# Prefix decays written to DRAM once per chunk, and a new order of the work, in an mLSTM layer with two MLPs

## The chip, the core and the metric

The kernel runs on one core of one Trainium2 chip. The metric is the device time of one execution in microseconds (us); three runs of the kernel before gave 461.3, 463.23 and 463.48 us, median 463.23.

## The reference

An mLSTM attention layer for 2 batches, 8 heads, 768 steps and head size 40 is followed by two MLPs (320 to 2048 to 320) over the 1536 tokens, the first with a hard-swish, the second with a mish.

```python
for t in range(S):
    m_new = np.maximum(f_gate[:, :, t] + m, i_gate[:, :, t])
    f_stab = np.exp(f_gate[:, :, t] + m - m_new)
    i_stab = np.exp(i_gate[:, :, t] - m_new)
    C = f_stab * C + i_stab * outer(vt, kt)
    n = f_stab * n + i_stab * kt
    y[:, :, t] = sigmoid(o_gate[:, :, t]) * (C @ qt) / np.maximum(np.abs(n . qt), 1.0)
x = y as (1536, 320)
h = x @ w1_in;  x = (h * clip(h + 3, 0, 6) / 6) @ w1_out
h = x @ w2_in;  out = (h * tanh(log1p(exp(h)))) @ w2_out
```

## The kernel before

The steps are cut into 6 chunks of 128 (`c` from 0 to 5); a chunk of one batch is a *unit* `(b, c)`. `gates(c)` (L665) transposes the gates of a chunk, forms the decay of each step, and with one scan along the chunk the product of the decays up to each step, the *prefix decays*: 16 rows (batch and head) of 128 values in `mt`. They go to a DRAM tile `pd` (L706 to 708), each row written 40 times, once for every element of a head, and come back per unit as `pb` (L773 to 777): 120 partitions (three heads of 40) in three groups, at rows 0, 120 and 200. `query` (L862) multiplies the transposed queries `q3` by `pb`, so that the product with the carried state `c` (L937, the tile `o`) has the decay since the chunk's start. The tiles `q3` and `pb` have one buffer each (`in_q3`), which L937 of the unit before sets free.

Of a unit, `scores` (L799) multiplies queries and keys (tile `s`), `decays` (L817) makes the 128 by 128 decay matrices of its 8 heads with a scan (tile `fb`; the row that it starts from is loaded from DRAM, `fz`, or for the first two chunks spread by TensorE at L831), `values` and `carry` (L844, L874) scale values and keys, form the state's new part (tile `st`, L888) and add it, and `unit` (L913) sums it all up in `o` (L937, L941), divides, gates, and transposes the result into the MLP's input `X` (tile `xp`).

The weights come as two pieces per slot of 256 features, `ri` (384 KiB each) and `ro` (320 KiB), into two raw buffers (`narrow`, L347, DMA at L357). Each piece is widened on ScalarE and VectorE (`top`, L365 and L367), rounded to the fast matmul's format on ScalarE (`wh`, `wd`) and has its remainder taken (`wl`, and the second half of `wd`) on VectorE, GpSimd or, where `pe_rest` says so, TensorE (`low_on_pe`, L384). The first MLP runs for chunks 0 and 1 in steps of 256 tokens (`ph` at L460, then `r`, `gh`, `gl`, then `acc` at L479), between the units of attention; for chunks 2 to 5 in steps of 512 tokens (`phw`, `accw`); then the second MLP (`qh`, `bcc`). Each of its steps is 8 matmuls up and 6 to 12 down.

All is recorded by a planner, `Flow` (L193): each task asks for an engine with an estimated duration, and the task with the lowest number in the table `P` goes first among those that are ready by the estimates. Every engine then runs its instructions in the order so recorded, and waits where the real durations differ. All DMAs are issued by SyncE (SP), in one row. Where TensorE has nothing to do by the estimates before the third unit's end, the planner puts products of zeros (`pz`, `fill` at L1122), which keep it busy.

Of the kernel before, what the change touches and what calls it, by code (L numbers as in the profile page):

```python
# [8 lines left out]
F32 = mybir.dt.float32  # L9
# [30 lines left out]


P = {
    "const": [140, 266, 278, 196, 64],
    "gates": [74, 143, 41, 167, 142, 225],
    "load": [233, 138, 177, 125, 222, 205, 154, 122, 158, 239, 102, 159],
    "score": [20, 32, 85, 37, 301, 314, 268, 110, 202, 161, 5, 223],
    "value": [72, 16, 305, 136, 251, 23, 197, 262, 248, 307, 117, 0],
    "carry": [105, 214, 215, 261, 67, 12, 260, 8, 137, 267, 9, 168],
    "unit": [96, 269, 232, 40, 124, 77, 257, 220, 38, 17, 242, 116],
# [8 lines left out]
    ],  # L58
    "down2": [
        203, 59, 171, 252, 4, 25, 156, 69, 6, 28, 147, 108, 180, 186, 34, 241, 35, 115, 80, 128, 55, 91,  # L60
        275, 19, 66, 18, 60, 224, 81, 86, 7, 151, 33, 118, 255, 250, 213, 30, 89, 73, 62, 53, 42, 56,
        134, 97, 319, 36,
    ],
    "half": [
        98, 13, 308, 263, 258, 221, 208, 279, 162, 39, 21, 298, 84, 240, 316, 112, 135, 90, 325, 54,
        119, 88, 201, 157,
    ],
    "wide1": [
        187, 150, 247, 297, 75, 99, 58, 153, 286, 169, 165, 245, 127, 193, 191, 277, 166, 270, 121, 284,
        139, 120, 311, 131, 285, 292, 68, 309, 306, 246, 276, 317,  # L70
    ],
    "down1w": [
        271, 289, 100, 148, 50, 101, 52, 65, 179, 234, 45, 173, 182, 175, 1, 238, 303, 94, 79, 57, 206,
        130, 43, 210, 61, 302, 172, 155, 93, 107, 82, 330,
    ],
    "drain": [322, 228, 326, 3, 27, 26, 2, 109, 76, 46],
    "now": [10, 14],
    "window": [0.01],


    "on_value": [1, 1, 1, 1, 0, 1, 0, 0, 0, 2, 0, 2],
    "on_key": [1, 2, 2, 1, 0, 1, 0, 1, 2, 1],
    "on_gate": [2, 1, 0, 1, 2, 0, 0, 0, 0, 0, 0, 0],
    "pool_query": [0, 0, 1, 0, 0, 0, 0, 0, 1, 0, 0, 1],
    "pool_state": [0, 0, 0, 1, 0, 0, 0, 0, 0, 0],
    "pool_rest": [
        1, 0, 1, 0, 0, 1, 0, 0, 1, 1, 0, 0, 0, 0, 1, 0, 0, 0, 0, 0, 0, 0, 0, 0, 0, 0, 0, 1, 1, 0, 0, 0,
    ],
    "pool_low": [
        0, 0, 0, 1, 0, 0, 1, 1, 0, 0, 0, 0, 0, 0, 0, 1, 1, 1, 0, 0, 0, 0, 0, 0, 0, 0, 1, 0, 1, 0, 0, 0,  # L90
        0, 0, 1, 0, 1, 1, 0, 1, 0, 0, 0, 0, 0, 0, 0, 0,
    ],

    "pe_rest": [0, 0, 0, 0, 0, 0, 0, 0, 0, 0, 0, 0, 0, 0, 0, 0],

    "pool_scan": [0, 0],

# [201 lines left out]
def mlstm_mlp_kernel(ctx, tc, qk, q3g, kvon, gates_io, w1i, w1o, w2i, w2o, eye, halves, consts, out):  # L299
# [368 lines left out]
    def gates(c):  # L668
        yield next(e for e, (_, z) in zip(scanned, SCANS) if c < z)
        yield have["ident"]  # L670
        q = slice(c * L, (c + 1) * L)
        yield in_a
        p = bank(f"pg{c}")
        yield PE, 0.21, 128
        T.transpose(p[:, 0:16], fgt[:, q], ident[:16, :16])
        T.transpose(p[:, 16:32], igt[:, q], ident[:16, :16])
        g = istab[c] = gpool.tile([128, 32], F32, tag=f"ist{c}", name=f"ist{c}")
        s = gpool.tile([128, 32], F32, tag=f"s{c}", name=f"s{c}")
        yield ACT, 0.16
        A.activation(s, p[:, 0:32], AF.Sigmoid, scale=-1.0)  # L680
        A.activation(g, p[:, 0:32], AF.Sigmoid)
        flow.put(in_a)
        yield DVE, 0.27
        V.reciprocal(out=s, in_=s)
        yield DVE, 0.1, True
        tt(V, g, g, s, ALU.mult)
        flow.set(gated[c])
        if c == 0:
            yield DVE, 0.03
            V.memset(g[0:1, 0:16], 0.0)  # L690
            flow.set(spreadable[c])
            return
        yield in_a
        pf = bank(f"pf{c}")
        yield PE, 0.11, 64
        T.transpose(pf[:16, 0:128], g[:, 0:16], ident)
        if P["spread"][c]:
            yield DVE, 0.03
            V.memset(g[0:1, 0:16], 0.0)
            flow.set(spreadable[c])  # L700
        yield ACT, 0.165
        A.copy(fgt[:, q], pf[:16, 0:128])
        yield DVE, 0.33, True
        V.tensor_tensor_scan(out=mt[:, q], data0=fgt[:, q], data1=fgt[:, q],
                             initial=1.0, op0=ALU.mult, op1=ALU.min)
        pd[c] = dpool.tile([16, D, L], F32, tag=f"pd{c}", name=f"pd{c}")  # L706
        yield SP, 330e3, rows_out[c][0]
        SY.dma_start(out=pd[c], in_=mt[:, q].unsqueeze(1).to_broadcast([16, D, L]))
        if not P["spread"][c]:
            yield DVE, 0.02  # L710
            V.memset(fgt[:, c * L : c * L + 1], 0.0)
            fzd[c] = dpool.tile([16, L], F32, tag=f"fz{c}", name=f"fz{c}")
            yield SP, 8e3, rows_out[c][1]
            SY.dma_start(out=fzd[c], in_=fgt[:, q])
        yield have["cst"]
# [13 lines left out]
    state = [gpool.tile([120, 3, 123], F32, tag=f"c{b}", name=f"c{b}") for b in range(B)]  # L729
    cnew = gpool.tile([120, 3, 123], F32, tag="cnew", name="cnew")  # L730
    units = [(b, c) for c in range(NC) for b in range(B)]
    got = {u: {k: Event() for k in ("qk", "kvo", "buf", "f", "q3", "p0", "p1")} for u in units}
    for u in units:
        got[u]["qk"] = Event(), Event()
    done = {u: {k: Event() for k in ("q3", "state", "o", "sig", "value")} for u in units}
# [4 lines left out]
    def loads(u, before):  # L740
# [29 lines left out]
        yield SP, 184e3, ev["q3"]  # L770
        SY.dma_start(out=t["q3"], in_=q3g[b, c])
        yield rows_out[c][0]
        rows = pd[c].rearrange("r e t -> (r e) t")[b * DM : (b + 1) * DM]  # L773
        yield SP, 123e3, ev["p0"]
        SY.dma_start(out=t["pb"][:, 0:2, :], in_=rows[0:240].rearrange("(g p) t -> p g t", g=2))
        yield SP, 61e3, ev["p1"]
        SY.dma_start(out=t["pb"][:, 2, :], in_=rows[200:320])

    def scaled(on, us, x, scale, n):

        if on == 2:
            yield ACT, H * (0.092 + 0.0007 * n)
            for h in range(H):
                A.mul(x[:, h, :], x[:, h, :], scale[:, h, :])
        else:
            yield flow.elementwise(on, us, H * n)
            tt(G if on else V, x, x, scale.to_broadcast([128, H, n]), ALU.mult)
# [9 lines left out]
    def scores(u):  # L797
        b, c = u
        t = tiles[u]  # L799
        for p in range(2):  # L800
            yield got[u]["qk"][p]
        yield got[u]["buf"]
        yield spreadable[c] if P["spread"][c] else got[u]["f"]
        yield in_pair
        yield in_a
        yield in_a
        flow.put(in_pair)
        sp = t["s"] = [bank(f"s{b}_{c}_{p}") for p in range(2)]
        yield PE, 1.06, 4096
        for h in range(4):  # L810
            for p in range(2):
                qke = t["qke"][64 * p : 64 * p + D]
                T.matmul(sp[p][:, h * L : (h + 1) * L], qke[:, 1, h, :], qke[:, 0, h, :], start=True, stop=True)  # L813
# [471 lines left out]
```

## Time and profile before

| | |
|---|---|
| median of three runs | 463.23 us |
| the profiled execution, its own time | 459.94 us |
| its span, first to last instruction | 458.2 us |
| TensorE busy (share of the span) | 441.1 us (96%) |
| VectorE, ScalarE, GpSimd busy | 317.7, 293.0, 54.1 us |
| DMA | 45.22 MB, of which 41.12 MB read from DRAM and 3.64 MB written |

The profile is of the one execution with its own time in the table; its span leaves out some 1.7 us around the instructions. A matmul's busy time is modelled and runs on into the next one's, so the distance between two starts tells what a matmul costs, and a busy TensorE may still run at half its clock: the granted clock is a row of its own. Single-precision matmuls appear as two records each, those in the fast format as one. SPq are the issue instructions of the DMA queue.

### The profile page before, as it was taken

To read this page: it belongs to the slowest core of one execution; us is meant where nothing else is said; L and a number is where in the kernel's file an instruction comes from. 1 tells how busy PE (TensorE), PEld (TensorE's weight loads), DVE (VectorE), ACT (ScalarE), POOL (GpSimd) and SP (SyncE) were. 2 spreads that over 40 slices of the span, in tenths; PEclk is the share of its full clock that TensorE was granted. 3 is DMA by queue.
4 is the path that set the end of the run, shared out by engine and by line. 5 is a ranking of instruction groups with operands and counts; after the bars stand their busy time and mean duration, and the time that the engine had idled before them with its cause. 6 is when DMAs were issued, how large, how long until landed. Compare 5 with 4: busy or idle time off the path is not lost.

```text
span 458.2 us, 7086 instructions
## 1 busy us (share of the span) xinstructions
PE 441.1 (96%) x2662; PEld 392.1 (86%) x2662; DVE 317.7 (69%) x552; ACT 293.0 (64%) x576; POOL 54.1 (12%) x53
## 2 busy tenths in 40 slices
PE   6987999699999999999999999999999999999996
PEld 5967999589999888888888888899989999889986
DVE  4796786669988777566555865766666666666665
ACT  4674683556747644766566666776777766767764
POOL 4323200132013301011024020000000000000000
PEclk9897899799999999999999999999999999999999
DMA  7768456895751652035203510000001000010001
GB/s 232 231 197 260 124 158 140 269 284 142 252 181 72 195 171 94 1 117 172 91 0 132 178 69 3 0 1 0 1 0 59 0 3 0 17 43 1 0 1 57
DMA packets 19636, 45.22 MB, mean 99 GB/s; under 512 B 1938, under 2 KB 11954, under 8 KB 19602
## 3 DMA queue, kind: packets, MB, share of 16 engines
q1 hardware_dynamic: 19602, 44.77, 31.1%
q8 instruction: 21, 0.34, 0.3%
q14 instruction: 13, 0.11, 0.1%
HBM read 41.12 MB, written 3.64 MB: 98 GB/s over the span
## 4 chain that ended last, share of the span: by engine, by line
PE 85%; DVE 5%; DMA 4%; ACT 2%; SPq 2%; issue 1%; POOL 0%; POOLq 0%; DVEq 0%; ACTq 0%
PE qh L460 19%; PE phw L460 13%; PE accw L479 13%; PE bcc L1091 6%; PE bcc L1090 6%; PE bcc L1089 6%; PE acc L479 5%; PE ph L460 5%; PE o L941 4%; PE s L813 2%; PE o L937 2%; DMA qke<-in_qk 1%; DMA pd<-mt 1%; PE st L888 1%; DMA ro<-in_w1o 1%; DMA pb<-pd 1%
## 5 line engine op out<-in xcount | busy, mean ns | idle before, releaser
L1091 PE MATMUL bcc<-wd,gl 128*128 128x320 f32 x192 | 59.3, 309 | 0.2 <-DVE gl L1046 0.2
L1089 PE MATMUL bcc<-wd,gh 128*128 128x320 f32 x192 | 59.3, 309 | 0.0
L1090 PE MATMUL bcc<-wd,gh 128*128 128x320 f32 x192 | 59.2, 309 | 0.0
L1040 DVE SCALAR_TENSOR_TENSOR u<-u,qh 128x512 f32<-128x512 f32 (+1 forms) x49 | 33.1, 676 | 36.8 <-ACT u L1038 36.8
L460 PE MATMUL qh<-xh,wh 128*128 128x512 f32 x144 | 56.8, 395 | 0.0
L460 PE MATMUL qh<-xl,wh 128*128 128x512 f32 x144 | 56.7, 393 | 0.0
L1036 ACT ACTIVATE u<-u,two 128x512 f32<-128x512 f32 (+1 forms) x49 | 35.1, 716 | 31.6 <-DVE u L1034 31.6
L479 PE MATMUL accw<-ghw,wd 128*128 128x512 f32 x160 | 52.2, 391 | 0.0
L1030 ACT ACTIVATE u<-qh 128x512 f32<-128x512 f32 (+1 forms) x49 | 28.7, 588 | 15.4 <-PE qh L460 15.4
L1089 PEld LDWEIGHTS bcc<-wd,gh 128*128 128x128 f32 x192 | 36.0, 188 | 2.1
L460 PE MATMUL qh<-xh,wl 128*128 128x512 f32 x96 | 37.7, 393 | 0.0
L460 PE MATMUL phw<-xh,wh 128*128 128x512 f32 x96 | 37.7, 393 | 0.0
L1090 PEld LDWEIGHTS bcc<-wd,gh 128*128 128x128 f32 x192 | 36.0, 188 | 1.9
L479 PE MATMUL accw<-glw,wd 128*128 128x512 f32 x96 | 37.5, 390 | 0.0
L479 PE MATMUL acc<-gh,wd 128*128 128x256 f32 x160 | 33.5, 295 | 4.1 <-ACT gh L549 4.1
L460 PE MATMUL phw<-xl,wh 128*128 128x512 f32 x96 | 37.4, 390 | 0.0
L1091 PEld LDWEIGHTS bcc<-wd,gl 128*128 128x128 f32 x192 | 36.0, 188 | 0.4 <-DVE gl L1046 0.4
L1046 DVE SCALAR_TENSOR_TENSOR gl<-u,gh 128x512 fp32r<-128x512 f32 (+1 forms) x49 | 33.1, 675 | 4.1 <-ACT gh L1044 4.0
L479 PEld LDWEIGHTS accw<-ghw,wd 128*128 128x128 f32 x160 | 29.8, 188 | 6.1
L1034 DVE SCALAR_TENSOR_TENSOR u<-u 128x512 f32<-128x512 f32 (+1 forms) x49 | 33.4, 682 | 1.6
L544 ACT ACTIVATE rw<-phw,half 128x512 f32<-128x512 f32 x32 | 22.0, 689 | 18.8 <-PE phw L460 15.1
L546 DVE SCALAR_TENSOR_TENSOR rw<-rw,phw 128x512 f32<-128x512 f32 x32 | 22.0, 686 | 16.3 <-ACT rw L544 16.2
(145 smaller groups left out, 1036.6 us busy)
## 6 DMA issues: line engine op xcount, KB each, us to landing
ri<-in_w1i SPq DMA_DIRECT2D x8, 768.0 KB
ri<-in_w2i SPq DMA_DIRECT2D x8, 768.0 KB
kvo<-in_kvon SPq DMA_DIRECT2D x12, 484.0 KB
ro<-in_w1o SPq DMA_DIRECT2D x8, 640.0 KB
ro<-in_w2o SPq DMA_DIRECT2D x8, 640.0 KB
fb<-fz SPq DMA_DIRECT2D x8, 512.0 KB
qke<-in_qk SPq DMA_DIRECT2D x24, 160.0 KB
out<-ot SPq DMA_DIRECT2D x12, 160.0 KB
```

The lines of the kernel that those rows point to most:

```text
L460: T.matmul(ph, a, b, start=(i == 0), stop=(i == len(seq) - 1))
L479: T.matmul(acc[k], a, b, start=start, stop=stop, skip_group_check=True)
L544: A.activation(r, ph, AF.Relu, bias=half, scale=1.0 / 6.0)
L546: V.scalar_tensor_tensor(out=r, in0=r, scalar=1.0, in1=ph, op0=ALU.min, op1=ALU.mult)
L1030: A.activation(u, ph, AF.Exp)
L1034: V.scalar_tensor_tensor(out=u, in0=u, scalar=2.0, in1=u, op0=ALU.add, op1=ALU.mult)
L1036: A.activation(u, u, AF.Ln, bias=two)
L1040: V.scalar_tensor_tensor(out=u, in0=u, scalar=0.5, in1=ph, op0=ALU.subtract, op1=ALU.mult)
L1046: V.scalar_tensor_tensor(out=gl, in0=u, scalar=-2.0, in1=gh.bitcast(F32), op0=ALU.mult, op1=ALU.subtract)
L1089: T.matmul(acc, a, hi, start=st, stop=False)
L1090: T.matmul(acc, a, lo, start=False, stop=False)
L1091: T.matmul(acc, b, hi, start=False, stop=sp)
```

## The change

It has three parts.

1. `pd` is now 16 rows of 128 values: one DMA of 8 KiB per chunk in place of one of 320 KiB. `pb` is loaded by three DMAs per unit (one per group) in place of two; each reads three rows of `pd`, every row 40 times by a step of zero, into 120 partitions. The bytes that arrive in `pb` are the same.
2. Two estimates of the planner: eight small ScalarE operations in `scaled` are now taken as 8 x (0.187 + 0.0007 n) us in place of 8 x (0.092 + 0.0007 n), and the scores count 2048 columns in place of 4096. The planner now also sees the three loads.
3. All numbers of the table `P` are new: the order, and where some operations run. `pe_rest` has two entries set (the first `ri` and the `ro` of slot 3 take their remainder on TensorE), `pe_low` one more, `pool_scan` one, and about as many operations as before are on GpSimd and on ScalarE's small scalings (7 each time).

```diff
-        pd[c] = dpool.tile([16, D, L], F32, tag=f"pd{c}", name=f"pd{c}")
-        yield SP, 330e3, rows_out[c][0]
-        SY.dma_start(out=pd[c], in_=mt[:, q].unsqueeze(1).to_broadcast([16, D, L]))
+        pd[c] = dpool.tile([16, L], F32, tag=f"pd{c}", name=f"pd{c}")
+        yield SP, 8e3, rows_out[c][0]
+        SY.dma_start(out=pd[c], in_=mt[:, q])
...
-        rows = pd[c].rearrange("r e t -> (r e) t")[b * DM : (b + 1) * DM]
-        yield SP, 123e3, ev["p0"]
-        SY.dma_start(out=t["pb"][:, 0:2, :], in_=rows[0:240].rearrange("(g p) t -> p g t", g=2))
-        yield SP, 61e3, ev["p1"]
-        SY.dma_start(out=t["pb"][:, 2, :], in_=rows[200:320])
+        rows = pd[c][b * H : (b + 1) * H]
+        for g in range(3):
+            yield SP, 61e3, ev[f"p{g}"]
+            src = rows[GBASE[g] : GBASE[g] + 3].unsqueeze(1).to_broadcast([3, D, L])
+            SY.dma_start(out=t["pb"][:, g, :], in_=src)
...
-            yield ACT, H * (0.092 + 0.0007 * n)
+            yield ACT, H * (0.187 + 0.0007 * n)
...
-        yield PE, 1.06, 4096
+        yield PE, 1.06, 2048
...
+        yield got[u]["p2"]
...
-    "pe_rest": [0, 0, 0, 0, 0, 0, 0, 0, 0, 0, 0, 0, 0, 0, 0, 0],
+    "pe_rest": [1, 0, 0, 0, 0, 0, 0, 1, 0, 0, 0, 0, 0, 0, 0, 0],
```

Two places of the order matter below. In the names, `s0_1` is unit (0, 1), `ph0_1` the first MLP's step for chunk 0 and slot 1; the number at a name's end is the program's count. A unit's eight matmuls of `s`, sixteen of a `ph` and of an `acc` are shown by their first or last row.

TensorE, from the scores of unit (0, 1) to its `o`, before (`o` is L937 and L941):

```order
L813 MATMUL s0_1_1_425<-qke0_1_293 128x128
L1122 MATMUL pz_151<-zeros_150 128x512 x12
L888 MATMUL st0_1_458<-kvo0_1_389 120x123 x3
L831 MATMUL fb1_1_0_479<-ident4_85,ist1_345 128x128 x4
L831 MATMUL fb1_1_1_480<-ident4_85,ist1_345 128x128 x4
L937 MATMUL o0_1_498<-c0_100,q30_1_398 128x123 x2
L941 MATMUL o0_1_498<-kvo0_1_389,fb0_1_395 128x41 x8
L813 MATMUL s1_1_0_510<-qke1_1_453 128x128
L460 MATMUL ph0_0_514<-xh0_92,wh0_0_123 128x256
L937 MATMUL o1_1_595<-c1_101,q31_1_531 128x123 x2
L941 MATMUL o1_1_595<-kvo1_1_476,fb1_1_478 128x41 x8
```

and now (the lines behind the change are one higher):

```order
L813 MATMUL s0_1_1_436<-qke0_1_312 128x128
L460 MATMUL ph0_0_453<-xh0_92,wh0_0_123 128x256
L1123 MATMUL pz_151<-zeros_150 128x512 x7
L831 MATMUL fb1_1_0_501<-ident4_85,ist1_358 128x128 x4
L460 MATMUL ph0_1_502<-xh0_92,wh0_1_129 128x256
L813 MATMUL s1_1_1_539<-qke1_1_483 128x128
L479 MATMUL acc0_541<-gh0_0_481,wd0_0_125 128x256 x2
L938 MATMUL o0_1_582<-c0_100,q30_1_415 128x123 x2
L942 MATMUL o0_1_582<-kvo0_1_401,fb0_1_412 128x41 x8
L831 MATMUL fb1_1_1_551<-ident4_85,ist1_358 128x128 x4
L889 MATMUL st0_1_526<-kvo0_1_401 120x123 x3
L938 MATMUL o1_1_677<-c1_101,q31_1_606 128x123 x2
```

Two steps up (`ph0_0`, `ph0_1`), the scores of unit (1, 1) and one step down (`acc`) now stand ahead of the first `o` that needs `pb`; before, filler, `st` and `fb` stood there, and the steps up came behind it. The next `o`, of unit (1, 1), is the last row shown: `fb`, `st` and two steps of 16 matmuls (`acc`, `ph0_2`) lie between.

SP, the loads around chunk 2's decays, before:

```order
L357 DMA ro1_0_751<-in_w2o 128x2560
L708 DMA pd2_749<-mt_99 640x1x128
L714 DMA fz2_770<-gio_98 16x128
L766 DMA fb0_2_675<-fz2_770 128x1024
L708 DMA pd4_834<-mt_99 640x1x128
L708 DMA pd3_838<-mt_99 640x1x128
L771 DMA q30_2_850<-in_q3g 120x384
L714 DMA fz4_860<-gio_98 16x128
L714 DMA fz3_872<-gio_98 16x128
L775 DMA pb0_2_851<-pd2_749 120x2x128
L777 DMA pb0_2_851<-pd2_749 120x128
L357 DMA ro0_5_904<-in_w1o 128x2560
```

and now:

```order
L357 DMA ro0_5_653<-in_w1o 128x2560
L357 DMA ri0_3_778<-in_w1i 128x3072
L357 DMA ro1_0_799<-in_w2o 128x2560
L708 DMA pd2_840<-mt_99 16x128
L708 DMA pd5_851<-mt_99 16x128
L714 DMA fz5_874<-gio_98 16x128
L708 DMA pd3_876<-mt_99 16x128
L766 DMA fb0_2_748<-fz2_858 128x1024
L714 DMA fz3_910<-gio_98 16x128
L771 DMA q30_2_930<-in_q3g 120x384
L777 DMA pb0_2_931<-pd2_840 120x1x128 x3
L357 DMA ri0_4_952<-in_w1i 128x3072
```

The weight piece `ro` of slot 5 stood behind three writes of `pd`, the writes of `fz` and the loads of `pb`; it now stands ahead of them all, and `ri` of slot 4 stands behind them. A `pd` has 16 rows instead of 640, a `pb` three loads.

## Rows read from the trace of the kernel before

**Rows 1.** The page: busy time by engine; granted TensorE clock in 40 slices, tenths.

```profile
PE 441.1 (96%) x2662; PEld 392.1 (86%) x2662; DVE 317.7 (69%) x552; ACT 293.0 (64%) x576; POOL 54.1 (12%) x53
...
PEclk9897899799999999999999999999999999999999
```

**Rows 2.** Busy time in a stretch (from:to, us, engines with instruction counts, granted clock, DMA share, GB/s).

```profile
40.00:50.00 10.00, 10.00 (x57) 9.70 (x57) 5.25 (x12) 2.96 (x7) 4.21 (x4) 0.53 0.50 169
```

**Rows 3.** Chain that ended last, 27 to 52 us: start, us, what.

```profile
27.07 5.86 DMA pd<-mt
...
33.36 3.92 DMA pb<-pd
...
37.44 1.53 POOL q L306
...
39.01 1.43 PE o L937 x6
40.45 3.34 PE o L941 x16
...
45.80 5.65 PE ph L460 x32
```

**Rows 4.** Timeline of TensorE in the same stretch: start, us, what, idle before it.

```profile
30.99 3.04 PE L1122 MATMUL pz<-zeros 128*128 128x512 f32 x12
...
34.50 1.95 PE L831 MATMUL fb<-ident,ist 128*128 128x128 f32 x16
39.01 1.43 PE L937 MATMUL o<-c,q 120*128 120x123 f32 x6 [2.56 <-POOL q L306]
```

**Rows 5.** Chain that ended last, 114 to 122 us, TensorE at full clock.

```profile
114.15 1.92 PE ph L460 x16
116.06 1.09 PE s L813 x16
...
119.26 0.63 PE st L888 x6
119.89 0.64 PE o L937 x6
120.53 1.75 PE o L941 x16
```

**Rows 6.** Timeline of SP, the DMA issues after writes of `pd`.

```profile
28.54 2.47 SPq L357 DMA_DIRECT2D ro<-in_w1o  x1
...
69.44 3.24 SPq L771 DMA_DIRECT2D q<-in_q3g  x1
72.78 4.01 SPq L714 DMA_DIRECT2D fz<-gio  x2
...
79.07 0.36 SPq L357 DMA_DIRECT2D ro<-in_w1o  x1
```

**Rows 7.** Timelines of ScalarE (first row) and TensorE, 83 to 92 us.

```profile
83.27 0.91 ACT L365 CAST top<-ro 128x640 f16<-128x640 bf16 x1 [5.67 <-DMA ro<-in_w1o]
...
84.70 0.80 PE L479 MATMUL acc<-gh,wd 128*128 128x256 f32 x2 [4.08 <-ACT gh L549]
...
89.57 2.31 PE L941 MATMUL o<-kvo,fb 128*128 128x41 f32 x16
```

**Rows 8.** The page: DMA packets of the whole run.

```profile
DMA packets 19636, 45.22 MB, mean 99 GB/s; under 512 B 1938, under 2 KB 11954, under 8 KB 19602
```

**Rows 9.** Two more stretches, columns as in rows 2.

```profile
72.00:74.00 2.00, 2.00 (x18) 1.98 (x18) 2.00 (x3) 0.20 (x1) 0.00 (x0) 1.00 0.70 89
...
172.00:173.00 1.00, 1.00 (x9) 0.77 (x6) 1.00 (x3) 0.00 (x0) 1.00 (x1) 1.00 1.06 428
```

**Rows 10.** Timelines of SP and VectorE: the first DMA's issue and its user.

```profile
0.73 0.73 SPq L1106 DMA_DIRECT2D gio<-in_gates_io  x1
...
2.93 0.47 DVE L658 TENSOR_TENSOR_SCAN mt<-gio,mt 16x128 f32<-16x128 f32 x1 [2.02 <-DMA gio<-in_gates_io]
```

**Rows 11.** Groups by line: the query product (busy us, mean ns, idle before).

```profile
L306 DVE TENSOR_TENSOR q<-q,pb 120x384 f32<-120x384 f32 x7 | 3.8, 546 | 6.0 <-DMA pb<-pd 6.0
```

More of the change, by code (lines that the diff above doesn't have):

```diff
@@ L42 @@
 P = {
[L43 to L49, printed above, removed]
[4 rows of a table removed]
+    "const": [265, 317, 315, 178, 133],
+    "gates": [21, 23, 84, 212, 267, 172],
@@ L54 @@
+    "load": [203, 239, 304, 202, 135, 258, 66, 54, 87, 19, 260, 63],
+    "score": [229, 183, 217, 134, 113, 75, 311, 121, 147, 112, 266, 218],
+    "value": [128, 41, 247, 153, 318, 242, 106, 167, 302, 28, 92, 287],
+    "carry": [206, 104, 288, 291, 86, 208, 143, 148, 8, 137, 149, 52],
+    "unit": [211, 82, 176, 10, 39, 150, 55, 295, 117, 200, 131, 96],
[4 rows of a table added]
     "up2": [
[3 rows of a table removed]
[3 rows of a table added]
     ],
     "down2": [
-        203, 59, 171, 252, 4, 25, 156, 69, 6, 28, 147, 108, 180, 186, 34, 241, 35, 115, 80, 128, 55, 91,
@@ L61 @@
-        275, 19, 66, 18, 60, 224, 81, 86, 7, 151, 33, 118, 255, 250, 213, 30, 89, 73, 62, 53, 42, 56,
-        134, 97, 319, 36,
+        226, 94, 42, 5, 49, 132, 190, 164, 111, 81, 74, 145, 26, 227, 38, 61, 234, 76, 37, 51, 45, 22,
+        3, 244, 27, 58, 72, 68, 184, 25, 162, 158, 278, 71, 136, 36, 241, 182, 233, 139, 163, 171, 69,
+        130, 213, 220, 102, 165,
     ],
     "half": [
-        98, 13, 308, 263, 258, 221, 208, 279, 162, 39, 21, 298, 84, 240, 316, 112, 135, 90, 325, 54,
-        119, 88, 201, 157,
+        48, 12, 186, 316, 289, 57, 210, 245, 98, 232, 204, 271, 31, 142, 105, 314, 16, 181, 215, 294,
@@ L67 @@
+        299, 324, 256, 127,
     ],
     "wide1": [
-        187, 150, 247, 297, 75, 99, 58, 153, 286, 169, 165, 245, 127, 193, 191, 277, 166, 270, 121, 284,
-        139, 120, 311, 131, 285, 292, 68, 309, 306, 246, 276, 317,
+        6, 32, 292, 205, 277, 83, 56, 319, 225, 14, 222, 320, 273, 236, 274, 114, 209, 180, 24, 297, 40,
+        95, 250, 261, 306, 207, 161, 269, 243, 20, 275, 251,
     ],
     "down1w": [
-        271, 289, 100, 148, 50, 101, 52, 65, 179, 234, 45, 173, 182, 175, 1, 238, 303, 94, 79, 57, 206,
@@ L74 @@
-        130, 43, 210, 61, 302, 172, 155, 93, 107, 82, 330,
-    ],
[L76 to L85, printed above, removed]
+        107, 77, 230, 116, 221, 264, 196, 17, 170, 293, 126, 85, 119, 65, 43, 144, 35, 118, 44, 93, 60,
@@ L86 @@
+        300, 272, 103, 2, 59, 101, 4, 47, 110, 285, 262,
+    ],
+    "drain": [122, 259, 67, 15, 109, 9, 1, 173, 99, 88],
+    "now": [11, 13],
+    "window": [0.05],
+    "on_value": [1, 2, 0, 1, 0, 0, 0, 1, 0, 0, 0, 0],
+    "on_key": [1, 2, 2, 0, 2, 1, 2, 1, 0, 0],
+    "on_gate": [0, 0, 0, 2, 0, 0, 2, 0, 0, 0, 0, 0],
+    "pool_query": [0, 0, 1, 0, 0, 0, 0, 0, 1, 1, 0, 0],
+    "pool_state": [0, 1, 1, 0, 0, 0, 0, 0, 0, 0],
     "pool_rest": [
-        1, 0, 1, 0, 0, 1, 0, 0, 1, 1, 0, 0, 0, 0, 1, 0, 0, 0, 0, 0, 0, 0, 0, 0, 0, 0, 0, 1, 1, 0, 0, 0,
+        0, 0, 0, 1, 0, 1, 0, 0, 0, 1, 0, 0, 0, 0, 0, 0, 0, 0, 0, 0, 0, 1, 1, 1, 1, 0, 0, 0, 0, 0, 0, 1,
@@ L88 @@
     ],
     "pool_low": [
-        0, 0, 0, 1, 0, 0, 1, 1, 0, 0, 0, 0, 0, 0, 0, 1, 1, 1, 0, 0, 0, 0, 0, 0, 0, 0, 1, 0, 1, 0, 0, 0,
-        0, 0, 1, 0, 1, 1, 0, 1, 0, 0, 0, 0, 0, 0, 0, 0,
-    ],
-    "pe_rest": [0, 0, 0, 0, 0, 0, 0, 0, 0, 0, 0, 0, 0, 0, 0, 0],
-    "pool_scan": [0, 0],
-    "pe_low": [0, 1, 0, 1, 0, 0, 0, 0, 0, 0, 0, 0],
+        0, 1, 0, 0, 1, 0, 0, 0, 0, 1, 1, 1, 0, 1, 0, 0, 1, 1, 0, 0, 0, 0, 0, 0, 0, 1, 0, 0, 0, 0, 0, 0,
+        0, 0, 1, 0, 0, 0, 0, 0, 0, 0, 0, 0, 0, 1, 0, 0,
+    ],
@@ L100 @@
+    "pe_rest": [1, 0, 0, 0, 0, 0, 0, 1, 0, 0, 0, 0, 0, 0, 0, 0],
+    "pool_scan": [1, 0],
+    "pe_low": [1, 1, 0, 1, 0, 0, 0, 0, 0, 0, 0, 0],
     "spread": [1, 1, 0, 0, 0, 0],
@@ L731, in mlstm_mlp_kernel @@
     units = [(b, c) for c in range(NC) for b in range(B)]
-    got = {u: {k: Event() for k in ("qk", "kvo", "buf", "f", "q3", "p0", "p1")} for u in units}
+    got = {u: {k: Event() for k in ("qk", "kvo", "buf", "f", "q3", "p0", "p1", "p2")} for u in units}
     for u in units:
```

14 rows, old and new, of the table P are left out of this document.

## The prediction

> **What bounds the kernel now.** I read the page first. TensorE is busy 96% of the span, and from the ninth of the 40 slices (about 92 us) on its clock stands at 9 tenths or more in every slice [rows 1]. So nothing is to be won behind that point but by taking matmuls away, and the change takes none of substance. What can be won lies in the first 92 us, and "busy" hides part of it: between 40 and 50 us TensorE is busy all the time at a clock of 0.53, the lower of its two levels (1.2 and 2.4 GHz) [rows 2].
>
> Then I followed the chain of waits and found two places.
>
> *Place one, 31 to 51 us.* The write of `pd` for chunk 1 takes 5.86 us, the second load of `pb` 3.92, the query product on GpSimd 1.53, and only then does the `o` of unit (0, 1) start, at 39.01 [rows 3]. TensorE meanwhile ran twelve fillers, `st`, the `fb` of the next unit, and stood idle for 2.56 us [rows 4]; what came after it ran at half the clock. From 30.99 to 51.45, that is 20.5 us, it did work that at full clock takes 9.9 us: `st` 0.63, `fb` 1.95, the state's product 0.64, `o` 1.75, the scores 1.09 and two steps up of 1.92 each, priced where the clock is full [rows 4, 5]. Lost: 10.6 us.
>
> *Place two, 80 to 92 us.* TensorE waits 4.08 us for a ScalarE result that stood in line behind a `top` copy, which waited 5.67 us for the weight piece `ro` of slot 5 [rows 7]. That piece was issued at 79.07. SP had been held up: the `q3` issue that follows two writes of `pd` lasts 3.24 us, the two `fz` issues after it 4.01, where such an issue takes 0.36 [rows 6]; the issue soon after the first `pd` is long too, 2.47 us. After the wait the work of 84.70 to 91.9 runs at half the clock: eight records of `acc` (0.96, as a `ph` of the same width), `st` 0.63, the state's product 0.64 and `o` 1.75 make 4.0 us of 7.2 [rows 5, 7]. Lost: 4.1 + 3.2 = 7.3 us.
>
> Together 17.9 us.
>
> **The change part by part.**
>
> *The new order at place one* puts two steps up, the next unit's scores and one step down ahead of the first `o`. The 10.6 us come back as far as these can run. A residue stays: the queries and keys of unit (1, 1) are issued behind three loads of `pb`, which wait for `pd`. `pd` can't be issued before about 28 us (27.07 now [rows 3]); give it 3 us to land and 2.3 for the issues behind it, and those loads leave at about 33.3. Their own landing takes 2.2 us at the least, the first DMA's time from issue to use [rows 10], and what a set of `pb` puts in front (next paragraph) comes on top: 40.5. TensorE, at 31 us behind the scores of (0, 1) as now, gets there after a step up 1.92, seven fillers 1.7 (twelve take 2.9 [rows 4]), half a `fb` 1.0 and a step up 1.92: 37.5. I count a wait of 3.0 us and 1.0 for the clock after it: **4.0**. The query product (GpSimd, 1.53 [rows 3], now behind the remainders of slot 1's `ro` there) is done by 42, and TensorE comes to its `o` at 40.5 + 1.09 + 1.92 = 43.5, so it stays hidden. Bounds: 0 (no load is in the way) and 6.8 (slow packets, below).
>
> *The narrow loads.* The page counts 1938 packets under 512 bytes [rows 8], and the program has 132 DMAs: 78 have an outer size that 16 divides, 30 have 120 partitions, 24 have 40. 78 x 16 + 30 x 15 + 24 x 10 = 1938 exactly, one closing packet per engine used. So a DMA runs on the largest number of engines, up to 16, that divides its outer size (the new program would show 78 x 16 + 10 x 15 + 24 x 10 + 30 x 3 = 1728). The new `pb` loads read an outer size of three: 120 packets of 512 bytes per engine and unit on three engines, where now 24 lie on each of 15. What a packet of 512 bytes costs is bounded by two stretches: in one filled by `pd` writes, 89 GB/s at a share of 0.70 of 16 engines, 7.9 GB/s each or 64 ns a packet; in one with large packets 428 GB/s at 1.06, 25 GB/s or 20 ns [rows 9]. A set of 120 takes 2.4 to 7.7 us; loads should be cheaper than writes, and I take the middle, 5.0.
>
> The Trainium skill, "DMA: Bandwidth & Descriptors", section "Why a DMA increments its semaphore by 16 and not by 1", says that the number of engines is the largest, up to 16, that divides the slowest dimension of both sides; by it 3 and 120 give three engines for each new load. The trace agrees with the rule for 16, 15 and 10; no run here shows three.
>
> *What they hold up.* `q3` and `pb` have one buffer, so from one unit's state product to the next at least this passes: two issues of 0.4 [rows 6], 2.2 to land [rows 10], 5.0 for the set, 0.55 for the product [rows 11]: 8.5 us. By the new order TensorE has between them, for units (0, 1) and (1, 1), `o` 1.75, `fb` 0.98, `st` 0.63, a step down and a step up of 1.92: 7.2 us [rows 4, 5]. In the same way 8.0, 7.7 and 8.3 for the pairs of chunks 2, 3 and 5; the rest have 10 or more. Waits: 1.3 + 0.5 + 0.8 + 0.2, rounded up **3.0**. With a set of 7.7 it would be 16; with 2.4 none. The third load costs SP another 0.4 us per unit, 4 us in all; it is hidden while TensorE has more than 8.5 us between units.
>
> *The short `pd`.* 40 packets per engine become one. That takes away the long issues of place two, and `ro` of slot 5 now stands ahead of all those DMAs anyway, so the 7.3 us come back. Next in line there is `ri` of slot 4 behind the loads of `pb`, and the keys and values of (1, 2). For what these come late I take **2.0** (an estimate: two waits of 1 us; bounds 0 and 4).
>
> *Work added to TensorE.* The remainder of slot 3's `ro` on TensorE: 640 columns in single precision at 1.95 us per 1024 [rows 4] and 640 in the fast format at 1.92 per 4096 [rows 5], 1.2 + 0.3 = **1.5**, in a dense stretch. The one of slot 0 falls among the start's fillers and counts nothing; its cover is gone only if the first scores come before about 10 us. One more `xp` remainder is 0.2, inside the rounding.
>
> *The start.* A weight piece is now the first DMA and its copies come first on ScalarE and VectorE. Its 393 KB at 428 GB/s are 0.9 us [rows 9], its conversion as much again, and both stand before the first gates: **2.0** (bounds 0, since the first scores wait for their own DMA, and 3).
>
> *The longer estimates* of small ScalarE operations cost and give nothing by themselves: seven groups of eight before and after.
>
> Sum: 17.9 - 4.0 - 3.0 - 2.0 - 1.5 - 2.0 = 5.4 us gained. The profiled execution took 459.9 us and would take 454.5. The median of the runs shown is 3.3 above it, so I forecast **457.8 us** against 463.2.
>
> **The rivals.**
>
> *The loads are cheap* (a packet near 20 ns, nothing waits): only start and added work are paid, 17.9 - 3.5 = 14.4, **448.8 us**. For it: a large packet moves at that rate. Against it: every stretch of 512-byte packets is far slower. The same page, section "Specifications", holds 512 bytes to be enough for full rate; rows 9 speak against that for writes.
>
> *The change doesn't do what it says at place two*: SP's long issues come from the sum of what is queued, not from `pd`, and the wait of 7.3 us stays in another spot. **465.1 us**, no change that can be told. For it: three loads put 120 packets on an engine where `pd` put 40, so the queue may fill as before. Against: `ro` of slot 5 is issued earlier.
>
> *Slower: the recurrence of `pb` sets the pace.* At 64 ns a set takes 7.7 us, the time between units 11.3, the waits 16 instead of 3 and the one at place one 6.8 instead of 4: 17.9 - 2 - 6.8 - 1.5 - 16 - 2 = -10.4, **473.6 us**. It decides from a set of 6 us on, 50 ns a packet, where the gain is gone. For it: the only stretch of pure 512-byte traffic. Against: that traffic is writes.
>
> **How the numbers follow.** A measurement can tell about 0.5%, 2.3 us. Forecast 0.41, cheap loads 0.22, no change 0.17, slower 0.20: faster 0.63, same 0.17, slower 0.20. The forecast's own range is 453 to 461. For 8 in 10 the whole one takes in the cheap loads at the low end and stops a little short of the slow packets: 448 to 470.
>
> **What would show it.** Right: no filler or idle TensorE between 31 and 41 us but a short wait at the scores of (1, 1); no issue of 2 to 4 us behind `pd`; `ro` of slot 5 landed before its copy is due; 1728 packets under 512 bytes. Wrong: waits of several us at the state's product of every second unit (slow packets), or the place-two wait again behind another weight piece. If the clock's row still has low slices after 60 us, the forecast is too good.

## The result, and the profile after

The changed kernel takes 456.46 us (median of 17 runs, 454.42 to 462.33), the kernel before 462.52 on the same chip (17 runs, 460.16 to 464.29): a ratio of 0.9893, 95% interval [0.9871, 0.9915]. It is 1.1% faster; 457.8 was forecast, in a range of 448 to 470. Single executions of either kernel scatter by several us, so a median holds more than one profile (ratios here and below leave out executions over 1.5% above the fastest of their kernel, medians don't): the profiled executions have their own times of 459.94 before and 458.0 after, and spans of 458.2 and 456.1 us. A last group of runs below shows one stall that some executions have and others don't.

The page of the changed kernel, against [rows 1, 8]:

```profile
PE 443.8 (97%) x2669; PEld 393.8 (86%) x2669; DVE 319.2 (70%) x552; ACT 293.4 (64%) x583; POOL 47.5 (10%) x48
PEclk9969799999999999999999999999999999999999
DMA packets 16307, 43.62 MB, mean 96 GB/s; under 512 B 1729, under 2 KB 8625, under 8 KB 16273
```

The clock's low slices end with the fifth of the 40 (57 us); before, the eighth still had one. 1729 packets under 512 bytes stand against 1728 forecast: the new loads do run on three engines each.

Stretches of 10 us (columns: stretch, length, busy time of each engine with its instructions, granted clock, DMA share, GB/s):

```profile
40.00:50.00 10.00, 6.76 (x42) 6.20 (x41) 6.91 (x8) 5.18 (x10) 4.90 (x5) 0.74 0.60 173
...
60.00:70.00 10.00, 9.27 (x68) 7.71 (x68) 7.60 (x22) 9.25 (x37) 0.00 (x0) 1.00 0.44 160
...
80.00:90.00 10.00, 10.00 (x91) 9.75 (x90) 9.06 (x15) 7.50 (x21) 3.02 (x1) 1.00 0.85 291
```

Place two (80 to 92 us) is gone: TensorE is busy at full clock. Place one has become a wait between 41 and 45 us with a slow stretch behind it. TensorE's timeline there, against [rows 4] (start, duration, and in brackets the idle time before it and what ended it):

```profile
41.20 0.28 PE L460 MATMUL ph<-xl,wh 128*128 128x256 f32 x1
43.97 0.46 PE L813 MATMUL s<-qke 40*128 40x128 f32 x2 [2.50 <-DMA qke<-in_qk]
45.17 2.04 PE L813 MATMUL s<-qke 40*128 40x128 f32 x14 [0.74 <-DMA qke<-in_qk]
47.14 0.79 PE L479 MATMUL acc<-gh,wd 128*128 128x256 f32 x2
...
50.72 1.23 PE L938 MATMUL o<-c,q 120*128 120x123 f32 x6
51.79 1.92 PE L942 MATMUL o<-kvo,fb 128*128 128x41 f32 x16
```

The wait stands where it was forecast, at the scores of unit (1, 1), and is 2.50 + 0.74 = 3.24 us long. The step down behind it takes 50.72 - 47.14 = 3.58 us, 1.92 at full clock. The chain of waits, against [rows 3], says what the queries and keys waited for:

```profile
30.57 5.20 DMA pd<-mt
...
35.79 0.83 SPq L777
...
36.68 0.74 SPq L777
...
37.47 0.89 SPq L777
...
38.93 6.11 DMA qke<-in_qk
```

8 KiB need 5.20 us to land here, hardly less than the 320 KiB before (5.86). The size of the write is not what sets this: in `e2` below, which has the same write in the old order, the loads of `pb`, which wait for it, leave 2.56 us after its issue. SP's timeline there:

```profile
30.09 0.33 SPq L708 DMA_DIRECT2D pd<-mt  x1
...
32.65 1.63 SPq L776 DMA_DIRECT2D pb<-pd  x2
```

In the changed kernel a weight piece `ro` stands in SP's row between the write and the loads. SP waits 3.4 us until VectorE's remainder (`wd`) has freed that piece's buffer, so the loads could not have left before 35.5 us however fast the write was:

```profile
30.57 0.37 SPq L708 DMA_DIRECT2D pd<-mt  x1
30.99 0.68 SPq L771 DMA_DIRECT2D q<-in_q3g  x1
35.15 0.35 SPq L357 DMA_DIRECT2D ro<-in_w1o  x1
35.79 2.56 SPq L777 DMA_DIRECT2D pb<-pd  x3
```

The three issues take 0.8 us each, where [rows 6] show 0.36 for an issue; the queries and keys behind them land 6.11 us after theirs. SP's timeline behind chunk 2's decays, against [rows 6]:

```profile
70.52 1.38 SPq L708 DMA_DIRECT2D pd<-mt  x2
72.00 1.14 SPq L714 DMA_DIRECT2D fz<-gio  x2
73.19 0.41 SPq L708 DMA_DIRECT2D pd<-mt  x1
```

The two `fz` issues behind two writes took 4.01 us before and take 1.14.

### The profile page after: what moved, and what is told of

The parts are those of the page before. It is cut to its first block, busy times and chain, and to the rows that moved or that the text cites. A ratio compares the mean times of both kernels' runs of the same rounds, so it can differ in the third digit from the quotient of the medians.

```text
span 456.1 us, 7107 instructions
## 1 busy us (share of the span) xinstructions
PE 443.8 (97%) x2669; PEld 393.8 (86%) x2669; DVE 319.2 (70%) x552; ACT 293.4 (64%) x583; POOL 47.5 (10%) x48
## 2 busy tenths in 40 slices
DMA packets 16307, 43.62 MB, mean 96 GB/s; under 512 B 1729, under 2 KB 8625, under 8 KB 16273
## 3 DMA queue, kind: packets, MB, share of 16 engines
HBM read 41.12 MB, written 2.04 MB: 95 GB/s over the span
## 4 chain that ended last, share of the span: by engine, by line
PE 79%; DMA 9%; DVE 4%; ACT 3%; issue 2%; SPq 1%; POOL 1%; DVEq 0%; POOLq 0%; ACTq 0%
PE qh L460 20%; PE phw L460 11%; PE accw L479 11%; PE bcc L1092 6%; PE bcc L1091 6%; PE bcc L1090 6%; PE acc L479 6%; PE o L942 4%; PE ph L460 4%; DMA fb<-fz 2%; PE s L813 2%; DMA kvo<-in_kvon 2%; DMA ri<-in_w2i 1%; DMA qke<-in_qk 1%; PE o L938 1%
## 5 line engine op out<-in xcount | busy, mean ns | idle before, releaser
L479 PE MATMUL accw<-glw,wd 128*128 128x512 f32 x96 | 37.5, 391 | 0.1
L460 PE MATMUL phw<-xl,wh 128*128 128x512 f32 x96 | 37.4, 390 | 0.0
```

Source lines behind the costliest of these rows:

```text
L460: T.matmul(ph, a, b, start=(i == 0), stop=(i == len(seq) - 1))
L479: T.matmul(acc[k], a, b, start=start, stop=stop, skip_group_check=True)
```

## The experiments

Theory A, the prediction's: place one comes back through the new order, place two through the short write and the earlier weight piece, and the narrow loads cost something. Rival B: the DMAs alone do it, and the order gives nothing. Rival C: the order would give more, but pays for the two remainders that it takes on TensorE. Every kernel here computes the whole result. The runs were made on several chips; the ratios below are to the kernel before on the same chip, with 95% intervals.

### Order and DMAs apart

`e1_new_order_old_dma` has the new order, and the old write and loads:

```diff
-        pd[c] = dpool.tile([16, L], F32, ...)
-        SY.dma_start(out=pd[c], in_=mt[:, q])
+        pd[c] = dpool.tile([16, D, L], F32, ...)
+        SY.dma_start(out=pd[c], in_=mt[:, q].unsqueeze(1).to_broadcast([16, D, L]))
...
```

> Theory A (the gain is the new order's; the DMA part gives nothing by itself): ratio to the kernel before 0.985 to 0.993, about the changed kernel's 0.989, and the wait of TensorE between 80 and 92 us stays away although SP shows issues of 2 to 4 us behind each write of pd. Theory B (the gain is the short write, which frees SP): ratio 0.995 to 1.005, with a wait of 3 us or more on a late weight piece or on late scores.

Measured: 1.005 [1.0011, 1.0088]. SP is held up again behind the writes, and a wait at place two is back although `ro` of slot 5 now stands ahead of them. What comes late this time is the row from which the decay scan starts (`fb` from `fz`); ScalarE's `gh`, for which TensorE waits, stands behind that scan. SP's timeline, then VectorE's (first row) and TensorE's:

```profile
68.58 1.61 SPq L708 DMA_DIRECT2D pd<-mt  x2
70.29 6.20 SPq L714 DMA_DIRECT2D fz<-gio  x2
...
78.18 2.63 SPq L766 DMA_DIRECT2D fb<-fz  x1
```

```profile
84.84 1.23 DVE L837 TENSOR_TENSOR_SCAN fb<-fb,ident 128x512 f32<-128x512 f32 x1 [5.94 <-DMA fb<-fz]
...
87.35 0.50 PE L479 MATMUL acc<-gh,wd 128*128 128x256 f32 x2 [2.99 <-ACT gh L549]
89.50 0.58 PE L479 MATMUL acc<-gl,wd 128*128 128x256 f32 x1 [1.65 <-POOL gl L306]
```

`e2_old_order_new_dma` has the old order (old table, old estimates), with the short write and the three narrow loads.

> Theory A: ratio 0.997 to 1.008; the wait at the first o stays, the loads of pb hold SP for 2.2 us per unit, and a weight piece or scores come late somewhere between 70 and 95 us. Theory B: ratio 0.985 to 0.992; the wait of 4.1 us at 80 us is gone because SP isn't held up behind pd.

Measured: 0.9822 [0.9776, 0.9869], 452.6 us, *better* than the whole change and below both ranges. SP and TensorE around place two:

```profile
66.96 0.77 SPq L708 DMA_DIRECT2D pd<-mt  x2
67.82 0.38 SPq L771 DMA_DIRECT2D q<-in_q3g  x1
68.36 0.77 SPq L714 DMA_DIRECT2D fz<-gio  x2
```

```profile
80.00:90.00 10.00, 10.00 (x88) 10.00 (x87) 8.96 (x16) 8.39 (x24) 5.49 (x4) 1.00 0.73 208
```

The q3 issue that took 3.24 us now takes 0.38. So place two is won by the short write alone. Theory A falls, since the order gives nothing by itself (e1), and rival B stands.

`e7_old_order_long_write_narrow_loads` keeps the old order and the long write, and takes the narrow loads from its first copy:

```diff
-        rows = pd[c].rearrange("r e t -> (r e) t")[b * DM : (b + 1) * DM]
+        rows = pd[c][b * H : (b + 1) * H, 0, :]
```

> The old order with the long write of pd as before (640 packets) and the new loads (three engines). If the two DMA costs add up, the narrow loads cost 0.9% on the long write as they do on the short one: ratio 1.005 to 1.013. If the narrow loads are hidden behind the long write's own delay: 0.998 to 1.004. If most of the gain came from the loads after all: below 0.995.

Measured: 1.0245 [1.018, 1.0311], 475.7 us, above all three ranges. It differs from e2 in the write alone. Its longest waits on TensorE (in total, times, longest):

```profile
PE acc L479 <- ACT gh L549: 6.7, 1, 6.7
PE s L815 <- DMA qke<-in_qk: 3.9, 2, 3.3
PE o L939 <- POOL q L306: 3.2, 1, 3.2
```

The wait of place two, 4.08 us before [rows 7], is 6.7; the other two were 2.2 and 2.6 us. Narrow loads behind long writes cost more than the two costs added up (1.009: 0.009 for narrow loads, e2 against e4 below, on top of 1 for the kernel before). These waits are 4.9 us longer than before, of the 12.7 us between the medians; the rest was not traced.

### Wide loads

`e3_new_order_15_engines` and `e4_old_order_15_engines` write the decays five times and read 15 rows 8 times each, so that a load has an outer size of 15:

```diff
-        pd[c] = dpool.tile([16, L], F32, ...)
-        SY.dma_start(out=pd[c], in_=mt[:, q])
+        pd[c] = dpool.tile([16, 5, L], F32, ...)
+        SY.dma_start(out=pd[c], in_=mt[:, q].unsqueeze(1).to_broadcast([16, 5, L]))
-            src = rows[GBASE[g] : GBASE[g] + 3].unsqueeze(1).to_broadcast([3, D, L])
+            src = rows[5 * GBASE[g] : 5 * GBASE[g] + 15].unsqueeze(1).to_broadcast([15, 8, L])
```

> pd written five times (80 packets), each load of pb from 15 rows, every one 8 times, so that by the count of small packets it runs on 15 engines. If the three-engine loads cost time: a set of three issues takes 1.2 us on SP in place of 2.2, the wait of 3.2 us at the scores of unit (1, 1) falls to under 1.5 us, and the ratio is 0.981 to 0.987 (1 to 3 us better than the changed kernel). If they are hidden: ratio 0.987 to 0.992. Packets under 512 bytes: 1938 + 150 = 2088.

> The old order with a short write and wide loads, so without either cost of the DMAs. Theory A: ratio 0.993 to 1.0; Theory B: 0.983 to 0.990. In both, the wait of 4.1 us at 80 us shrinks to under 2 us if SP's long issues came from pd, and stays if they came from the sum of what is queued.

Measured: e3 0.9831 [0.9787, 0.9874], e4 0.9729 [0.9679, 0.9779], 448.1 us, below both of its ranges. The wait of place two is 0.3 us in e4. The intervals of e2 and e4 just touch, as do those of the changed kernel and e3; on one chip e2's six executions took 449.5 to 454.7 us, e4's 446.8 to 451.4. The small packets of e3 are 2088 = 1728 + 30 x 12, as the count by outer sizes has it, and the wait at the scores of (1, 1) shrinks from 3.2 to 0.3 us. One part missed: a set's issues did not get shorter, 2.6 us for three. So it is the time to land that narrow loads lengthen. From the first issue of a set to a `q` that waited for it, the changed kernel takes 5.5 to 9.2 us (five sets), e4 4.5 and 5.6 (two sets). TensorE's waits for `q` (in total, times, longest) show what that costs, in e2 (two rows) and e4:

```profile
PE o L939 <- DVE q L306: 2.4, 2, 1.6
PE o L939 <- POOL q L306: 1.1, 2, 0.8
...
PE o L941 <- DVE q L306: 1.2, 1, 1.2
```

### Is it the work added to TensorE?

`e5_slot3_remainder_on_dve` and `e6_both_remainders_on_dve` are the changed kernel with the remainder of slot 3, or of slots 0 and 3, on VectorE in the same place of the order.

```diff
+            on_dve = s == 3
...
-            T.matmul(ps, ident, src, start=True, stop=False)
-            T.matmul(ps, minus, hi, start=False, stop=True)
+            if not on_dve:
+                T.matmul(ps, ident, src, start=True, stop=False)
+                T.matmul(ps, minus, hi, start=False, stop=True)
...
+                    tt(V, dst, src[rows, c], hi[rows, c].bitcast(F32), ALU.subtract)
```

> The changed kernel with slot 3's remainder on VectorE at the same place of the order (four matmuls on TensorE and four copies on ScalarE less, four subtractions on VectorE more). Theory C (the new order gives back 3 us of the DMA's gain through the work it adds to TensorE and ScalarE between 60 and 70 us): ratio to the kernel before 0.980 to 0.986, TensorE's lost time between 60 and 75 us falls by 1 us or more beside the 1.5 us of work. Theory D (it gives it back elsewhere, at the start or in later waits): 0.987 to 0.991.

> As the run before, and slot 0's remainder on VectorE too. If slot 0's matmuls only take the place of fillers, as the forecast counted: the same ratio as with slot 3 alone, within 0.003. If they cost their 1.6 us: 0.003 to 0.005 lower. If VectorE is on the path at the start: higher.

Measured: 0.9926 [0.9891, 0.996] and 0.9984 [0.995, 1.0018]: no gain, and with both a loss (the changed kernel has 0.9893 [0.9871, 0.9915]). e5 lies above its two ranges, and e6 above e5, which was the sign set for VectorE being on the path. What TensorE is spared returns as waits for VectorE (e6: `o` for `fb` 2.3 us, once). Rival C falls in this form.

### The write from ScalarE's queue

`e8_old_order_15_engines_write_from_act` and `e9_new_order_15_engines_write_from_act` are e4 and e3 with the write issued by ScalarE, `e10_old_order_narrow_loads_write_from_act` is e2 with it (there the short write, in the same way):

```diff
-        SY.dma_start(out=pd[c], in_=mt[:, q].unsqueeze(1).to_broadcast([16, 5, L]))
+        A.dma_start(out=pd[c], in_=mt[:, q].unsqueeze(1).to_broadcast([16, 5, L]))
```

> The old order with wide loads, the write of pd issued by ScalarE and so on another queue than all other DMAs. If the write of chunk 1 lands late because it stands behind other transfers in SP's queue (5 us from issue to landing with 8 KiB as with 320): it lands in 2 to 3 us, the lost time between 30 and 60 us falls by 1.5 to 3 us, ratio 0.966 to 0.970. If the engines themselves are full: no change, 0.971 to 0.976. If the issue holds ScalarE up: above 0.976.

> The new order with the wide loads, and the small write of the decays issued by ScalarE's queue, so that it no longer stands behind the loads in SyncE's row. If the order itself costs what it has cost in the three pairs so far (0.7 to 1.0% against the old order with the same DMAs): ratio 0.977 to 0.981 to before, against the 0.969 of the old order with the same DMAs. If the order was only late because the decays of chunk 1 landed late in it (write issued at 30.6 us, landed 5.2 us later), that goes with this edit, the two orders meet, ratio 0.966 to 0.972, and the wait at the scores of unit (1, 1) is gone.

> The old order with the short write of 16 rows issued by ScalarE, and the three narrow loads kept. It tells the two gains of the best kernel so far apart. If the landing of the decays is what the write from ScalarE gives, it gives the same here as with wide loads, 0.3 to 0.5% beside the 0.9822 of the same kernel with the write in SyncE's row: ratio 0.977 to 0.980. If narrow loads wait in any case for their 120 packets on three engines, nothing moves: 0.981 to 0.984.

Measured: e8 0.9692 [0.9641, 0.9744], 448.3 us; e9 0.9869 [0.9814, 0.9923]; e10 0.9883 [0.9789, 0.9977]. e8's ratio lies where it was expected of a faster landing: its loads of `pb` leave 2.9 us after the write's issue, e4's 4.0 us. e9 and e10 lie above all their ranges. In no pair do the intervals lie apart, and two of three changed for the worse: who issues the write is not shown to matter. With wide loads the two orders do not meet (e9 against e8), and the trace says why the write's queue can't help there: in e9 SP waits 4.3 us at the `ro` between, issues it at 35.39 and the loads right behind it at 35.82; they do not wait for the write at all.

The profile of e10 showed something else. TensorE lost some 9 us at the last unit, (1, 5), which e2 does not lose. SP's, GpSimd's and TensorE's timelines, and a stretch:

```profile
157.52 1.47 SPq L776 DMA_DIRECT2D pb<-pd  x2
159.04 0.69 SPq L779 DMA_DIRECT2D pb<-pd  x1
159.78 0.68 SPq L357 DMA_DIRECT2D ri<-in_w2i  x1
160.50 0.43 SPq L357 DMA_DIRECT2D ro<-in_w2o  x1
...
167.14 0.99 POOL L306 TENSOR_TENSOR q<-q,pb 120x384 f32<-120x384 f32 x1 [21.95 <-DMA pb<-pd]
168.19 1.57 PE L939 MATMUL o<-c,q 120*128 120x123 f32 x6 [4.35 <-POOL q L306]
169.55 3.55 PE L943 MATMUL o<-kvo,fb 128*128 128x41 f32 x16
```

```profile
170.00:175.00 5.00, 5.00 (x20) 4.61 (x20) 1.79 (x6) 0.62 (x1) 0.00 (x0) 0.50 0.00 0
```

The set comes into use 9.6 us after its first issue. TensorE waits 4.35 us for it and comes back at the lower clock (`o` 3.55 us where 1.92 is usual). This is the forecast's slower rival, at one unit. In e2, the same set is used 5.6 us after its issue:

```profile
161.63 1.47 SPq L776 DMA_DIRECT2D pb<-pd  x2
...
167.18 1.01 POOL L306 TENSOR_TENSOR q<-q,pb 120x384 f32<-120x384 f32 x1 [17.81 <-DMA pb<-pd]
168.24 0.90 PE L939 MATMUL o<-c,q 120*128 120x123 f32 x6 [0.23 <-POOL q L306]
```

`e11_last_chunk_wide_rest_narrow` is e10, but makes chunk 5's write and loads wide (the loads are shown); `e12_narrow_loads_write_from_act_again` is e10 unchanged, on e11's chip.

```diff
+        if c == NC - 1:
+            return rows[5 * GBASE[g] : 5 * GBASE[g] + 15].unsqueeze(1).to_broadcast([15, 8, L])
         return rows[GBASE[g] : GBASE[g] + 3].unsqueeze(1).to_broadcast([3, D, L])
```

> The old order with the short write from ScalarE and narrow loads, but chunk 5's decays written five times and loaded in the wide form, 15 rows of which each is read 8 times. In the profile of the same kernel with narrow loads throughout, the last set (issued at 157.5 us) came into use 9.6 us later, in place of 5.6 in the kernel whose write is in SyncE's row; TensorE stood idle 4.35 us for it and then ran at half its clock until about 178, some 9 us in all. If the narrow set is what is late there, the last set is used 4.4 to 5 us after its issue, the wait is gone, and the runs stand near the lower group of the other kernel's (452 us, ratio 0.975 to 0.980) with a smaller spread. If the delay comes from the two weight pieces issued behind the set, the wide set waits as well, and the runs spread over 452 to 465 as before.

> The old order with the short write from ScalarE and narrow loads once more, unchanged, beside the kernel with a wide last chunk on the same chip. Six executions gave 452.1, 452.5, 457.9, 458.1, 462.1 and 465.5 us. If late narrow sets make this spread, it shows again (10 us or more between fastest and slowest) and the median lies 4 to 8 us above the kernel with the wide last chunk. If the spread was that chip's, both kernels agree within 2 us.

Measured: e11 451.9 us median (450.16 to 456.65), ratio 0.9837 [0.9785, 0.989]; e12 456.82 (452.92 to 462.0), 0.9893 [0.9841, 0.9944]. The profiled execution of e12 has the same stall; in e11 it is gone, with the weight pieces issued right behind the set as before:

```profile
161.45 1.47 SPq L776 DMA_DIRECT2D pb<-pd  x2
...
170.36 0.99 POOL L306 TENSOR_TENSOR q<-q,pb 120x384 f32<-120x384 f32 x1 [21.21 <-DMA pb<-pd]
171.41 1.45 PE L939 MATMUL o<-c,q 120*128 120x123 f32 x6 [3.65 <-POOL q L306]
```

```profile
158.38 1.75 SPq L785 DMA_DIRECT2D pb<-pd  x2
...
161.05 0.55 SPq L357 DMA_DIRECT2D ri<-in_w2i  x1
162.69 1.07 POOL L306 TENSOR_TENSOR q<-q,pb 120x384 f32<-120x384 f32 x1 [16.63 <-PE s L824]
```

8.9 us in e12, 4.3 in e11, where the product waited for TensorE's scores last and not for the set. So the narrow set was what was late, in both profiles of that kernel. That the form of the loads matters fits the other profiles with the old order: wide sets at this place are used 4.4 us after their first issue (e4, e8), narrow ones after 5.6 (e2), 7.2 (e7), 8.9 and 9.6.

Why the same set came in 5.6 us in e2 stays open. The single DMA packets in the traces give a hint: 5 us after the first issue 359 of e2's 360 packets of 512 bytes have started, but 323 of e10's and 316 of e12's. The others follow until 9.1 and 8.3 us, while packets of the two weight pieces run. In e10 and e12 a load of 8 KiB of instructions (0.69 and 0.31 us) starts 2.1 and 2.7 us after the first issue, in e2 none before 8.2 us. e8 and e11 have one at 1.9 us too, and the last packet of their wide sets starts by 3.9 us. But e7's narrow set has none either, and 332 packets. So what causes the delay is not shown.

The medians of e11 and e12 differ by 4.9 us, as expected, but their intervals overlap, and e11's ratio lies above its range. In how many of the unprofiled executions the set was late stays open as well. The scatter does not tell: e12 and e10 scatter over 9.1 and 13.4 us and e11 over 6.5, but so does the kernel before on the same chips, over 11.7 and 10.5 (11 executions each), without narrow loads.

### All together

| write and loads | old order | new order |
|---|---|---|
| long write, two loads | 1 (before) | 1.005 (e1) |
| short write, narrow loads | 0.9822 (e2) | 0.9893 (the change) |
| five copies, wide loads | 0.9729 (e4) | 0.9831 (e3) |
| the same, write from ScalarE | 0.9692 (e8) | 0.9869 (e9) |

In every row the new order is slower, by 0.5% to 1.8%. In the second and the last row the two kernels were not run side by side; each ratio is to the kernel before that ran beside it. The best kernels, e4 and e8 (448.1 and 448.3 us), have the old order; they beat the kernel before and the change.

## Why the prediction was right, and where it was wrong

The number was right and the side as well; the credit was given to the wrong part, and some sizes were off. To hold the forecast's terms against the profiled pair I take for either trace the lost time as the prediction did: time elapsed, less TensorE's work at full-clock prices. It grows as follows (us):

| stretch | before | after | gained by | the term | forecast |
|---|---|---|---|---|---|
| 0 to 30 | 16.3 | 16.4 | -0.1, and 1.7 of added work: -1.8 | start | -2.0 |
| 30 to 60 | 12.7 | 10.5 | 2.2 | place one, 10.6 - 4.0 | 6.6 |
| 60 to 80 | 1.5 | 4.4 | -2.9, and -1.6 | what comes late; slot 3's remainder | -2.0; -1.5 |
| 80 to 95 | 7.2 | 0.1 | 7.1 | place two | 7.3 |
| 95 to 185 | 5.9 | 6.0 | -0.1 | waits between units | -3.0 |
| sum | 43.6 | 37.4 | 6.2 - 3.3 = 2.9 | | 5.4 |

The spans differ by 2.1 us. The medians differ by 6.1: the profiled execution of before was 2.6 us faster than its median over 17 runs, that of after 1.5 slower. So 457.8 against 456.46 is partly luck, since the pair of traces bears out half of the forecast's gain. The stretches are of time, not of work, and a row can be off by about 1 us.

**Place two: right in size, half right in cause.** 7.1 of 7.3 us came back. The prediction gave two reasons, the short write and the earlier `ro` of slot 5. e1 has the early `ro` and waits again, e2 has no early `ro` and doesn't. What SP loses behind long writes it loses for whatever stands behind them. The rival that put SP's long issues down to the sum of what is queued falls with e2, which has three loads to a set and short issues.

**Place one: the step that failed** is "The 10.6 us come back as far as these can run", with its residue of 4.0. Two terms of it were too small. The seven fillers that the prediction put in TensorE's way run from 36.90 to 38.51, 1.6 us that the residue left out. The clock behind the wait was put at 1.0, and it cost 1.1 on the scores (2.04 for 14 of 16, 0.95 at full price), 1.7 on the step down and 0.4 on the state's product: 3.2. With the wait of 3.24 that is 8.0, above the upper bound of 6.8.

That the wait itself was 3.24 where 3.0 was forecast is luck: its two ends came 4.0 and 4.5 us late. TensorE was done with the scores of (0, 1) at 34.88, 3.9 us later than before, where the forecast took 31 as before; so it stood ahead of those of (1, 1) at 41.5 and not at 37.5. The queries and keys landed at 45.0 and not at 40.5, since `pd` was issued at 30.57 (28 forecast) and landed after 5.20 us (3 forecast), and the `ro` that stands ahead of the loads was not in the sum.

Another 2.5 us are lost elsewhere in 30 to 60 us; e1 and e3, with loads that aren't narrow, lose only 6.7 and 6.3 there. So the new order does shorten place one (e1 against before), but gives it back: e1 is slower than before all the same. The pair e8 and e9 does not show it: counted in the same way, e9 loses some 1.5 us more there than e8. Of that price the traces show slot 3's remainder (two halves of 0.71 and 0.91 us where 1.5 was forecast), 1.7 us more for slot 0's and an `xp`, which the prediction counted at nothing under the start's fillers, and 2.9 in 60 to 80 us, where ScalarE is busy 9.25 of 10 us, with the gates of several chunks among its work; that this is the cause was only argued. SP's waits at the `ro` ahead of the loads (3.4 us in the changed kernel, 3.7 in e3, 4.3 in e9, under 0.7 in e2 and e4) are one more part. Which of these an order could do without was not settled: e5 and e6 moved the work and found no gain.

**The narrow loads: mechanism right, size about right, cost misplaced.** Three engines per load, by 1729 small packets where 1728 were forecast. The Trainium skill, "DMA: Bandwidth & Descriptors", section "Why a DMA increments its semaphore by 16 and not by 1", is borne out for three as well. A set was to take about 7.6 us from its first issue to use (0.4 + 2.2 + 5.0) and took 5.5 to 9.2. Of that, 120 packets were taken at 42 ns each, between 20 and 64; in the traces a packet of the narrow sets takes 28 to 33 ns, a packet of `pd` in the stretch of [rows 9] 64. But the waits between units (3.0) are not in the changed kernel's profile: no `o` waits there for its `q`. The set of unit (1, 1), issued at 52.42, is used at 58.41, and TensorE comes to that `o` at 59.20, 8.5 us behind the one before, where 7.2 was forecast. In e2, behind place one, they are there: 1.6, 0.8 and 0.2 us, and in e4 once 1.2. In the changed kernel the price shows in place one, through the queries and keys, and in the 0.6% and 0.9% that wide loads gain (e3, e4). The cheap loads (448.8) did not come by the narrow form; with wide loads and the old order the time is about that, by another sum.

**The slower rival** was real at one unit, the last one in e10 and e12. e7 has its time (475.7 us against 473.6) but not its mechanism: there `o` waits for its `q` 3.2 us in place one and 0.6 us once later, not at every second unit, and the longest wait is that of place two.

## What to carry to other kernels

Where many small packets are written from one queue, look at what that queue issues *next*: the cost here was not the write but single issues of 2.5 to 3.7 us behind it, by which unrelated loads came late. Look as well at what stands in that row between a write and the load that needs it: a piece that waits for its buffer holds up both. When data are spread by a step of zero, choose the outer size so that many engines share the load; here five copies in DRAM in place of one cost less than they gave. Test a new order and the edit that came with it apart: together they hid that one of them was a loss.

## What had not been expected of the hardware

- A small write is not always quick, and its queue alone does not decide it: issued by SP, 8 KiB landed after 2.5 us in e2 and after 5.2 in the changed kernel; issued by ScalarE, after 2.6 us in e10 and 4.6 and 4.7 in e11 and e12. 320 KiB took 5.5 to 6.1 us (e7, before, e1).
- A load with a step of zero took 0.7 to 0.9 us to issue (three: 2.2 to 2.6), a plain one of the kernel before 0.36 or 0.43, and 15 rows instead of 3 made it no shorter (0.82 to 0.96 mostly).
- The long write and the narrow loads together cost more than the sum: short write with wide loads 0.9729, short write with narrow loads 0.9822, long write with the old loads 1, both bad ones 1.0245 where the sum would be 1.009.
- One narrow set, with the same DMAs ahead of and behind it in the queue, came into use after 5.6 us in one kernel and after 8.9 and 9.6 in another that differs in who issues the small writes.
